# Keys and queries transposed on VectorE instead of TensorE, with values and scores set apart

## The chip, the core and the metric

The kernel runs on one core of a Trainium2 chip. The metric is the device time of one execution in microseconds (us), as the median over runs. Short names for the engines: PE is TensorE (PEld its weight loads), DVE is VectorE, ACT is ScalarE, POOL is GpSimd, SP is SyncE, whose queue issues nearly all DMAs here.

## What is computed

Batch B = 4, H = 8 heads, S = 768 tokens, D = 64 per head, all float32. First an attention in which each token sees a window of its neighbours (less than 16 away) and, for every block of 32 tokens, one summary key and one summary value; then a Fourier mixing layer with a two-layer MLP.

```python
k_sum = k.reshape(B, H, nb, 32, D).max(axis=3)
v_sum = v.reshape(B, H, nb, 32, D).mean(axis=3)
scores = concat(masked(q @ k.T / 8), q @ k_sum.T / 8 + log(32))
x = softmax(scores) @ concat(v, v_sum)            # heads side by side: (B, S, 512)
u = x + real(fft(fft(x, axis=1), axis=2))
out = u + relu(layernorm(u) @ w_ch1) @ w_ch2      # 512 -> 2048 -> 512
```

## The kernel before

**Stages.** The work goes batch by batch. For a batch b the program runs the attention (`gen_attention`, x of the batch), the Fourier mixing and normalisation (`gen_fourier`, whose result `u` holds the transposed, normalised rows) and the MLP: `gen_hidden(b, c)` (L1253) forms eight hidden layers j in two halves c, `gen_out(b, c)` (L1301) multiplies each half by the second weights. Both use a Strassen-like scheme: seven products X, Y, Z on sums and differences of quarter matrices. Matmuls named hx, hy, hz (L1268) are the hidden ones, ox, oy, oz (L1333) the output ones. Every product in float32 shows up in the trace as two passes per matmul, transposes as one.

**Overlap.** The attention of batch b+1 is spread among the MLP products of batch b. Generators do this: each `yield` ends a trip, and `drive` (main program, L1448) runs the generators by given rates: `(most, 44)` for the MLP of batch b, 74 for `gen_attention(b + 1)`. The trips give the program order; the tile framework then fixes one order per engine, in which each engine runs strictly, with semaphores for what it must wait for. The MLP of batch 0 runs beside the conversion of the weights from float64 (tiles `words`, on DVE and ACT) and beside batch 1's attention; there are four pairs of heads g per batch, and (b, g) names one.

**One pair of heads.** `load` (L574) fetches the keys and the queries of the pair, one DMA for each of the tiles kn and qn, with tokens on partitions, into a pool of four buffers (two pairs). `prepare` (L678) transposes them: for batches above 0, two groups of three PE transposes per tile (qk, L699) into PSUM, each followed by two copies on ACT (L701) into `kt` and `qt`, where partitions are the head dimension; then a block maximum of the keys on DVE (`km`, L706). `scores` (L757) makes 48 small matmuls (sc, L765), exponentials on ACT and a mask product on DVE (p); `sum_scores` (ss, L781) does the same for the block keys. `values` (L784) forms the weighted values: a small product vs (L788), which DVE spreads into the tile `vs`, 48 small matmuls (av, L798), 6 that use `vs` (L803), and on DVE a reciprocal and a scaled write into x. `load_values` fetches the values of a later pair in four DMAs (vw, 64 partitions by 12 pieces of 256 bytes); `block_sums` fetches four pieces of v (vb) into the one buffer called "room" and has POOL add them up.

In `gen_attention` (L949) a trip around the loop goes: values of the pair before, scores of this pair, both in one go; then loads; some empty trips; `prepare` of the next pair; `load` of the pair three ahead; more empty trips.

**Weights.** `get_w1` and `get_w2` fetch the seven-part weight tiles (w<-dw) two hidden layers ahead into three and four buffers. In batch 1 the first four second-weight tiles (w2 of j = 0 to 3) come with four parts only; DVE forms the other parts (four additions `w<-w`) and a DMA writes them back (dw<-w).

**PSUM.** Dense products rotate over four banks, attention over four others. An accumulating bank is read by DVE or ACT (`tt`, L566, or a copy) between two of its products, so PE waits where such a read is late: of hx, for instance, the last product of a layer needs DVE's addition `h<-hx,h` to have finished.

Of the kernel before, what the change touches and what calls it, by code (L numbers as in the profile page):

```python
# [490 lines left out]
def _main_program(ctx, tc, q, k, v, moe_w_ch1, moe_w_ch2, out):  # L491


    nc = tc.nc
    B, H, S, D = q.shape
# [5 lines left out]
    NP = H // 2  # L501
# [49 lines left out]
    def fetch(out, in_):  # L551

        ins = nc.sync.dma_start(out=out, in_=in_)
        if in_order[0]:
            tc.keep_in_program_order(ins)
# [16 lines left out]
    nat, marks = {}, {}  # L572

    def load(b, g, *which):  # L574

        for n in which or (1, 0):
            t = nat[b, g, n] = apool.tile([P, 2, NST // 2, 2 * D], FP, tag="nat", bufs=4, name=f"{'qk'[n]}n_{b}_{g}")
            fetch(out=t.rearrange("p e j n -> p (e j) n"),
                  in_=(q, k)[n][b, 2 * g:2 * g + 2].rearrange("e (j p s) d -> p (e j) (s d)", p=P, s=2))

# [60 lines left out]
    def load_values(b, g):  # L641
        if is_wide(b):
            load_wide_values(b, g)
            return
        if g % 2 and following(b, g, 1) and (b, g) != (1, 1) and not (b > 1 and g == 1):
            block_sums(*divmod((b * NP + g + 1) // 2, NP // 2))
        load_narrow_values(b, g)
# [30 lines left out]
    def prepare(b, g, *which):  # L678
        qn, kn = (nat[b, g, n] for n in range(2))
        kt, km = kt_bufs[g % 2], km_bufs[g % 2]  # L680
        qt = apool.tile([P, S], FP, tag="qt", name=f"qt_{b}_{g}") if 0 in (which or (0,)) else None
        for n in which or (1, 0):
            src, dst = (kn, kt[:, W:W + S]) if n else (qn, qt)
            if is_wide(b):
                for j0, j1 in ((0, 2), (2, 3)):
                    n = 2 * P * (j1 - j0)
                    ps = bank([P, n], f"qk_{b}_{g}_{j0}")
                    for j in range(j0, j1):
                        for s in range(2):
                            for e in range(2):  # L690
                                nc.tensor.matmul(ps[D * e:D * (e + 1), 2 * P * (j - j0) + s:2 * P * (j - j0 + 1):2],
                                                 src[:, e, j, D * s:D * (s + 1)], ident, start=True, stop=True)
                    nc.scalar.copy(out=dst[:, 2 * P * j0:2 * P * j1], in_=ps)
            else:
                for e in range(2):

                    ps = abank([P, S2], f"qk_{b}_{g}_{e}")
                    for j in range(NST // 2):
                        nc.tensor.transpose(ps[:, P * j:P * (j + 1)], src[:, e, j, :], ident)  # L699
                    for s in range(2):  # L700
                        nc.scalar.copy(out=dst[D * e:D * (e + 1), s:S:2], in_=ps[D * s:D * (s + 1)])  # L701
        if which == (0,):
            nat[b, g] = qt
            return
        with tc.issue_after(marks["fold", 0]) if (b, g) == (1, 0) else ExitStack():
            nc.vector.tensor_reduce(out=km[:, 0:nb], in_=kt[:, W:W + S].rearrange("p (n f) -> p n f", f=BLOCK),  # L706
                                    op=ALU.max, axis=AX.X)
        nat[b, g] = qt
# [48 lines left out]
    def scores(b, g):  # L757
        kt, qt = kt_bufs[g % 2], nat[b, g]
        ps = [abank([P, NB2, BLOCK], f"sc_{b}_{g}_{h}") for h in range(2)]
        for i in range(NB2):  # L760
            for h in range(2):
                o = BLOCK * (NB2 * h + i)
                for e in range(2):
                    rows, r = slice(D * e, D * (e + 1)), 64 * (e ^ h)
                    nc.tensor.matmul(ps[h][r:r + 64, i, :], kt[rows, o:o + 64], qt[rows, o:o + BLOCK],  # L765
                                     start=True, stop=True)
        p = apool.tile([P, 2, NQ, QB], FP, tag="p", name=f"p_{b}_{g}")
        pm = p[:, 1].rearrange("p n c -> p (n c)")[:, 0:S2]
        p = p[:, 0].rearrange("p (h i) (j c) -> p h (i j) c", h=2, c=BLOCK)
        for h in range(2):  # L770
            nc.scalar.activation(out=p[:, h], in_=ps[h], func=AF.Exp, scale=SC)  # L771
            tt(p[:, h], p[:, h], near[:, h], ALU.mult)
        return p, pm

    def sum_scores(b, g, p):
        km, qt = km_bufs[g % 2], nat[b, g]
        ps = abank([P, S2], f"ss_{b}_{g}")
        for h in range(2):
            for e in range(2):
                rows, r = slice(D * e, D * (e + 1)), 64 * (e ^ h) + 32 * h  # L780
                nc.tensor.matmul(ps[r:r + 32, :], km[rows, :], qt[rows, S2 * h:S2 * (h + 1)], start=True, stop=True)  # L781
        nc.scalar.activation(out=p, in_=ps, func=AF.Exp, scale=SC)
# [32 lines left out]
    def following(b, g, n):  # L815
        i = b * NP + g + n
        return divmod(i, NP) if i < B * NP else None
# [131 lines left out]
    def gen_attention(b):  # L949
        x = bpool.tile([P, NST, DM], FP, tag="x", bufs=2, name=f"x_{b}")  # L950
        x_of[b] = x
        held, pause = None, 1 if b == 1 else 5
        for g in range(NP + 1):
            if held:
                values(b, g - 1, *held, x)
            if g < NP:
                held = scores(b, g)
                sum_scores(b, g, held[1])
            if g and (n1 := following(b, g, 1)):
                load_values(*n1)  # L960
            if g == 1 and b > 1:
                block_sums(b, 1)
            if g == NP and b > 1:
                turn_tiles(b, x)
                for _ in range(12):
                    yield
                rooms[b] = room(f"fold_{b}")
                steps = fold_batch(b, split_fold(b, rooms[b]))
                while True:
                    with tc.issue_after(marks["dense"]):  # L970
                        done = next(steps, steps) is steps
                    if done:
                        break
                    yield
            if g == NP:
                return
            for _ in range(pause):
                yield
            n1, n3 = (following(b, g, n) for n in (1, 3))
            if n1 and b == 1:  # L980
                prepare(*n1)
            elif n1:
                prepare(*n1, 1)
                for _ in range(pause // 2):
                    yield
                prepare(*n1, 0)
            if n3:
                load(*n3)
            for _ in range(pause if b == 1 else pause - pause // 2):
                yield  # L990


# [396 lines left out]
    for vw in vw_bufs:  # L1389
        nc.gpsimd.tensor_copy(out=vw[:, :, D].rearrange("p (e n) -> p e n", e=2),  # L1390
                              in_=count[:, None, :].to_broadcast([P, 2, NQ]))

    def chain(*gens):
        for gen in gens:
            yield from gen
# [43 lines left out]
    for b in range(B):  # L1439


        most = chain(gen_hidden(b, 0), gen_out(b, 0), gen_hidden(b, 1))
        if b == 0:
            in_order[0] = False
            drive((most, 5, 0), (weights, 15, 0), (attn, 1, 0))
            done_weights.append(True)
        else:
            drive((most, 44, 0), (gen_attention(b + 1) if b + 1 < B else iter(()), 74, 0))  # L1448
        last = gen_out(b, 1)
        if b + 1 < B:  # L1450
            drive((gen_fourier(b + 1), 22, 600), (last, 12, 0))
        else:
            drive((last, 1, 0))
        if b == B - 2:

            ok = apool.tile([P, B * NP * 2 * NST], FP, tag="qt", name="ok")
            all_ok = spool.tile([P, 2], FP, tag="all_ok", name="all_ok")
            flag = cpool.tile([1, 1], I32, name="flag")
            rv = rec.rearrange("p n h i -> p (n h i)")
            nc.vector.tensor_scalar(out=ok, in0=rv, scalar1=1.0 / LIM, scalar2=None, op0=ALU.is_ge)  # L1460
            nc.vector.scalar_tensor_tensor(out=ok, in0=rv, scalar=LIM, in1=ok, op0=ALU.is_le, op1=ALU.mult)
            nc.vector.tensor_reduce(out=all_ok[:, 0:1], in_=ok, op=ALU.min, axis=AX.X)
            nc.vector.memset(all_ok[:, 1:2], 1.0)
            ps = bank([1, 1], "flag_ps")
            nc.tensor.matmul(ps, all_ok[:, 0:1], all_ok[:, 1:2], start=True, stop=True)
            nc.vector.tensor_scalar(out=flag, in0=ps, scalar1=P - 0.5, scalar2=None, op0=ALU.is_lt)
# [40 lines left out]
```

## Time and profile before

| | |
|---|---|
| median of 3 runs | 814.14 us (813.08 to 815.66) |
| the profiled execution | 820.64 us, of which the span in the trace is 818.8 us |
| mean granted PE clock | 0.981 of full speed |
| PE busy | 793.2 us, 97% |
| PE weight loads | 581.6 us, 71% |
| DVE busy | 492.6 us, 60% |
| ACT busy | 252.0 us, 31% |
| POOL busy | 46.2 us, 6% |
| DMA packets | 102332, 121.85 MB; 50768 under 512 bytes |
| qk transposes (L699), kn and qn | 72 each, 288 and 286 ns, 11.2 and 10.9 us busy |
| copies of them on ACT (L701) | 48 each for kt and qt, 506 and 504 ns |
| DMA issues of kn and qn | 16 each, 384 KB |

A line of the timeline reads: start in us, length of the group in us, engine, line of the program, operation, output<-inputs, shapes, and how many instructions it merges; brackets at its end hold the engine's idle time ahead of it and what released it, where "issue" means that it waited for nothing the profile shows. Matmuls are pipelined and their ends are modelled, so the spacing from start to start tells more than the length. In the DMA view, packets are single contiguous pieces; a share of 100% means that all 16 DMA engines' time is taken, and it can read above that where packets overlap.

### The profile page before, as it was taken

The page shows a single profiled execution, that of the slowest core. Times are in us where ns is not written, and L with a number is a line of the kernel's source. Part 1 is how long each engine was busy: PE and PEld are TensorE (multiplying, and loading weights), DVE is VectorE, ACT ScalarE, POOL GpSimd, SP SyncE. Part 2 cuts the span into 40 slices and gives each one's busy share as a digit, 9 for nine tenths or more (in the row PEclk, how much of TensorE's full clock was granted, in tenths as well). Part 3 has the DMA queues.
Part 4 walks back from the last instruction along what each step waited for, and adds up shares of the span by engine and source line. Part 5 has one row for each costly group of instructions (what it writes and reads, how often), then busy time and mean ns, then how long its engine had stood idle before and what let it go on. Part 6 is the DMA issues. An engine that isn't in the chain of part 4 may idle for free.

```text
span 818.8 us, 14635 instructions
## 1 busy us (share of the span) xinstructions
PE 793.2 (97%) x5998; PEld 581.6 (71%) x5998; DVE 492.6 (60%) x1121; ACT 252.0 (31%) x549; POOL 46.2 (6%) x85
## 2 busy tenths in 40 slices
PE   8969899999999999999999999999999999999997
PEld 6768665545579865688669876688659875786686
DVE  5767999887997753453577723364566723532351
ACT  3523765543635132411126114320116202001200
POOL 0010000000000310000030300000120000000000
PEclk9959999999999998999999999999999999999999
DMA  9998699788734376744614256411614044205001
GB/s 201 229 207 172 161 311 295 169 260 249 248 135 145 116 256 157 169 116 103 251 42 149 78 194 185 92 47 35 243 39 152 26 160 163 90 1 224 1 27 54
DMA packets 102332, 121.85 MB, mean 149 GB/s; under 512 B 50768, under 2 KB 83760, under 8 KB 102064
## 3 DMA queue, kind: packets, MB, share of 16 engines
q1 hardware_dynamic: 100992, 118.52, 50.2%
q0 software_dynamic: 576, 2.10, 0.8%
q8 instruction: 49, 0.80, 0.4%
q10 hardware_dynamic: 688, 0.20, 0.1%
q14 instruction: 27, 0.22, 0.1%
HBM read 97.22 MB, written 23.59 MB: 148 GB/s over the span
## 4 chain that ended last, share of the span: by engine, by line
PE 89%; DVE 4%; ACT 3%; DMA 2%; issue 1%; SPq 0%; DVEq 0%
PE hx L1268 20%; PE ox L1333 17%; PE hz L1268 10%; PE oz L1333 8%; PE o L1310 5%; PE hy L1268 5%; PE oy L1333 4%; PE y L1168 4%; PE sc L765 2%; PE mx L1127 2%; PE unt L1246 1%; PE av L798 1%; PE qk L699 1%; PE av L803 1%; PE ss L781 1%; DMA words<-in_v_dram 1%
## 5 line engine op out<-in xcount | busy, mean ns | idle before, releaser
L1268 PE MATMUL hx<-u,w 128*128 128x384 f32 x512 | 187.1, 493 | 0.3 <-ACT h L1279 0.2
L1268 PEld LDWEIGHTS hx<-u,w 128*128 128x128 f32 x512 | 95.1, 191 | 68.1 <-issue 3.6
L1268 PE MATMUL hz<-u,w 128*128 128x384 f32 x256 | 93.8, 489 | 0.0
L1333 PE MATMUL oz<-w,s 128*128 128x256 f32 x336 | 80.8, 379 | 0.0
L1333 PE MATMUL ox<-w,s 128*128 128x256 f32 x336 | 80.3, 380 | 0.0
L1333 PE MATMUL ox<-w,h 128*128 128x256 f32 x336 | 79.0, 380 | 1.0 <-DVE x L566 1.0
L566 DVE TENSOR_TENSOR x<-ox,x 128x256 f32<-128x256 f32 x84 | 35.2, 422 | 68.5 <-PE ox L1333 68.1
L1268 PEld LDWEIGHTS hz<-u,w 128*128 128x128 f32 x256 | 48.9, 192 | 34.6 <-issue 1.1
L1333 PEld LDWEIGHTS ox<-w,h 128*128 128x128 f32 x336 | 63.1, 190 | 10.5 <-DVE x L566 1.4
L1333 PEld LDWEIGHTS ox<-w,s 128*128 128x128 f32 x336 | 63.0, 190 | 9.9 <-issue 1.2
L1333 PEld LDWEIGHTS oz<-w,s 128*128 128x128 f32 x336 | 63.4, 190 | 8.7 <-DVE x L566 0.3
L1279 ACT COPY h<-hx 128x384 f32<-128x384 f32 x32 | 15.3, 479 | 143.1 <-PE hx L1268 143.0
L566 DVE TENSOR_TENSOR h<-hx,h 128x384 f32<-128x384 f32 x32 | 17.8, 555 | 55.7 <-PE hx L1268 55.7
L566 DVE TENSOR_TENSOR h<-hy,h 128x384 f32<-128x384 f32 x32 | 17.8, 555 | 50.1 <-PE hy L1268 48.1
L1268 PE MATMUL hy<-u,w 128*128 128x384 f32 x128 | 47.0, 488 | 0.6 <-issue 0.6
L1310 PE MATMUL o<-w,h 128*128 128x512 f32 x96 | 42.3, 595 | 0.0
L771 ACT ACTIVATE p<-sc 128x384 f32<-128x384 f32 x24 | 10.7, 488 | 95.1 <-PE sc L765 77.4
L1333 PE MATMUL oy<-w,h 128*128 128x256 f32 x168 | 39.9, 379 | 0.0
L1295 ACT ACTIVATE h<-hx 128x384 f32<-128x384 f32 x32 | 15.7, 491 | 70.1 <-PE hx L1268 70.0
L1268 PEld LDWEIGHTS hy<-u,w 128*128 128x128 f32 x128 | 24.0, 190 | 17.2 <-issue 1.2
L566 DVE TENSOR_TENSOR x<-oz,x 128x256 f32<-128x256 f32 x42 | 17.7, 422 | 30.1 <-PE oz L1333 29.8
L1333 PEld LDWEIGHTS oy<-w,h 128*128 128x128 f32 x168 | 31.9, 190 | 4.3
(162 smaller groups left out, 1147.1 us busy)
## 6 DMA issues: line engine op xcount, KB each, us to landing
w<-dw SPq DMA_DIRECT2D x44, 896.0 KB, 5.6
words<-in_moe_w_ch_dram SPq DMA_DIRECT2D x32, 512.0 KB, 6.1
dw<-w SPq DMA_DIRECT2D x12, 896.0 KB, 7.2
vw<-in_v_dram SPq DMA_DIRECT2D x47, 192.0 KB, 5.8
kn<-in_k_dram SPq DMA_DIRECT2D x16, 384.0 KB, 5.5
qn<-in_q_dram SPq DMA_DIRECT2D x16, 384.0 KB, 6.5
out_dram<-x SPq DMA_DIRECT2D x24, 256.0 KB, 2.5
vb<-in_v_dram SPq DMA_DIRECT2D x24, 192.0 KB, 4.2
```

Source lines behind the costliest of these rows:

```text
L566: return nc.vector.tensor_tensor(out=out, in0=in0, in1=in1, op=op).ins
L699: nc.tensor.transpose(ps[:, P * j:P * (j + 1)], src[:, e, j, :], ident)
L765: nc.tensor.matmul(ps[h][r:r + 64, i, :], kt[rows, o:o + 64], qt[rows, o:o + BLOCK], start=True, stop=True)
L771: nc.scalar.activation(out=p[:, h], in_=ps[h], func=AF.Exp, scale=SC)
L781: nc.tensor.matmul(ps[r:r + 32, :], km[rows, :], qt[rows, S2 * h:S2 * (h + 1)], start=True, stop=True)
L1127: nc.tensor.matmul(out, y[:, g], table, start=False, stop=True, skip_group_check=True)
L1168: nc.tensor.matmul(y, fgs[b][par][:, st, P * g:P * (g + 1)], fs[par][:, g % 2, st, :], start=(st == 0), stop=(st == n - 1))
L1268: ins = nc.tensor.matmul(ps, w[:, a, kk, :], u[:, r, kk, :], start=start and kk == 0, stop=stop and kk == 1, skip_group_check=True)
L1279: nc.scalar.copy(out=c11, in_=X)
L1295: nc.scalar.activation(out=c21, in_=X, func=AF.Relu)
L1310: nc.tensor.matmul(ps, h[:, n, hf, P * t:P * (t + 1)], wt[2, b, j][:, 2 * hf:2 * hf + 2, :], start=(n, hf) == (0, 0), stop=(n, hf) == (NC ...
L1333: nc.tensor.matmul(ps, left[a][:, n, :], wt[2, b, j][:, r, :], start=start and n == 0, stop=stop and n == NC - 1, skip_group_check=True)
```

## The change

From pair (2, 1) on, that is for the seven pairs (2, 1) to (3, 3):

- `load` brings each tile as four DMAs of 32 partitions, in which a partition receives 24 pieces of 32 floats (128 bytes): token 32 m + r of a head goes to partition r, block m. Each head fills two groups of 32 partitions, one for each half of its dimension.
- `prepare` turns the tile with one DVE transpose of 128 by 768 elements, which transposes each 32 by 32 block, straight into `kt` or `qt`. The PE transposes and ACT copies of these pairs go.
- Pairs (2, 1) and (2, 2) are no longer loaded during batch 1's attention but at the start of `gen_attention(2)`.
- In batches 2 and 3, values and scores of a loop turn lie three trips apart, `load_values` follows the values, and the empty trips are spread otherwise; the fold of the finished x starts after 17 trips instead of 12; the rate in `drive` is 76 instead of 74.

```diff
@@ load
+            if (b, g) > (2, 0):
+                t = nat[b, g, n] = t.rearrange("p e j n -> p (e j n)").rearrange("p (m c) -> p m c", c=32)
+                for e in range(2):
+                    for h in range(2):
+                        r, o = D * e + 32 * h, (q, k)[n][b, 2 * g + e].offset + 32 * h
+                        fetch(out=t[r:r + 32], in_=bass.AP((q, k)[n].tensor, o, [[D, 32], [32 * D, S // 32], [1, 32]]))
+                continue
@@ prepare
+            if (b, g) > (2, 0):
+                with tc.issue_after(marks["dense"]):
+                    nc.vector.transpose(out=dst, in_=src.rearrange("p m c -> p (m c)"))
+                continue
@@ gen_attention
-        held, pause = None, 1 if b == 1 else 5
+        held = None
+        if b == 2:
+            load(2, 1)
+            load(2, 2)
         for g in range(NP + 1):
+            n1, n3 = (following(b, g, n) for n in (1, 3))
             if held:
                 values(b, g - 1, *held, x)
-            if g < NP:
-                held = scores(b, g)
-                sum_scores(b, g, held[1])
-            if g and (n1 := following(b, g, 1)):
-                load_values(*n1)
-            if g == 1 and b > 1:
-                block_sums(b, 1)
+                if n1 and b > 1:
+                    load_values(*n1)
             if g == NP and b > 1:
                 turn_tiles(b, x)
-                for _ in range(12):
+                for _ in range(17):
                     yield
...
+            elif held and b > 1:
+                yield
+                yield
+                yield
+            if g < NP:
+                held = scores(b, g)
+                sum_scores(b, g, held[1])
+            if g and n1 and b == 1:
+                load_values(*n1)
+            if g == 1 and b > 1:
+                block_sums(b, 1)
+            if g == NP and b > 1:
+                return
+            yield
             if g == NP:
                 return
-            for _ in range(pause):
-                yield
-            n1, n3 = (following(b, g, n) for n in (1, 3))
-            if n1 and b == 1:
-                prepare(*n1)
-            elif n1:
-                prepare(*n1, 1)
-                for _ in range(pause // 2):
-                    yield
-                prepare(*n1, 0)
-            if n3:
+            if b > 1:
+                yield
+                yield
+            if n1:
+                prepare(*n1, *((1,) if b > 1 else ()))
+            if b > 1:
+                yield
+                yield
+                if n1:
+                    prepare(*n1, 0)
+            if n3 and not (b == 1 and n3 > (2, 0)):
                 load(*n3)
-            for _ in range(pause if b == 1 else pause - pause // 2):
+            yield
+            if b > 1:
                 yield
@@ main
-            drive((most, 44, 0), (gen_attention(b + 1) if b + 1 < B else iter(()), 74, 0))
+            drive((most, 44, 0), (gen_attention(b + 1) if b + 1 < B else iter(()), 76, 0))
```

## The prediction

> **What bounds it now.** I read the page first, engine shares and then the chain that ended last. VectorE (DVE) is busy 60%, ScalarE (ACT) 31%, so neither sets the end; TensorE (PE) does:
>
> ```profile
> PE 793.2 (97%) x5998; PEld 581.6 (71%) x5998; DVE 492.6 (60%) x1121; ACT 252.0 (31%) x549; POOL 46.2 (6%) x85
> PE 89%; DVE 4%; ACT 3%; DMA 2%; issue 1%; SPq 0%; DVEq 0%
> ```
>
> A busy share hides slow matmuls, so I took PE's timeline in the two stretches that hold the changed work, 290 to 392 us (batch 2's attention among batch 1's layers) and 481 to 579 us (batch 3's among batch 2's), and read start to start. From the first:
>
> ```profile
> 300.42 0.82 PE L699 MATMUL qk<-ident,kn 128*128 128x128 f32 x6
> 301.27 1.56 PE L1268 MATMUL hx<-u,w 128*128 128x384 f32 x4
> 302.67 0.82 PE L699 MATMUL qk<-ident,qn 128*128 128x128 f32 x6
> 303.32 1.46 PE L1268 MATMUL hx<-u,w 128*128 128x384 f32 x4
> ...
> 308.97 1.20 PE L798 MATMUL av<-vw,p 64*32 64x65 f32 x96
> 310.10 0.94 PE L803 MATMUL av<-vs,p 64*128 64x130 f32 x12
> 310.97 0.94 PE L765 MATMUL sc<-qt,kt 64*64 64x32 f32 x49
> 313.56 1.50 PE L765 MATMUL sc<-qt,kt 64*64 64x32 f32 x47 [1.65 <-issue]
> 315.00 1.50 PE L781 MATMUL ss<-qt,km 64*32 64x384 f32 x8
> 316.43 2.93 PE L1268 MATMUL hx<-u,w 128*128 128x384 f32 x4
> 319.15 2.01 PE L1268 MATMUL hz<-u,w 128*128 128x384 f32 x4
> 320.99 2.74 PE L1268 MATMUL hx<-u,w 128*128 128x384 f32 x8
> ```
>
> Two things cost PE time. Six transposes of one tile take 0.65 us (302.67 to 303.32). And at 311.9, in the middle of a score group, PE stops 1.65 us, then runs at half speed: four hidden passes take 2.72 us (316.43 to 319.15) where 1.29 is usual. It waits for no engine ("issue"). The DMA view of 312 to 316 us shows what is around it:
>
> ```profile
> DMA packets 2457, 0.63 MB, mean 158 GB/s; under 512 B 2456, under 2 KB 2456, under 8 KB 2456
> ## 3 DMA queue, kind: packets, MB, share of 16 engines
> q1 hardware_dynamic: 2456, 0.61, 127.2%
> q8 instruction: 1, 0.02, 2.2%
> ```
>
> The rings are full of 256-byte packets of values, with one fetch of instructions among them.
>
> [...] one 16 KB packet on q8; values and scores side by side are 212 passes, each with its weight load, so over 400 instructions in 4.3 us, and the stop lies inside them. [...] the array runs at half clock [...] (granted clock 0.50 from 315 to 320 us). [...]
>
> **Part 1: transposes off PE.** Seven pairs, (2,1) to (3,3), two tiles each: 14 groups of 6. At 0.65 us plus one 0.2 us bubble (300.42 to 301.27): 14 x 0.655 + 0.2 = **-9.4 us**, all on the bound engine. 56 copies of ACT go too (L701, 504 ns: 28 us), off the path; ACT has 31%.
>
> **Part 2: values and scores apart.** With four hidden products between them the burst of instructions halves. That should remove the stop: 310.97 to 323.57 is 12.60 us; the same passes at usual pace (1.53 + 0.78 + 1.29 + 1.29 + 2.58, bubble 0.1) are 7.57: **-5.0**. In the second stretch three smaller ones: 495.22 to 496.92 (1.70 for 1.29), 524.47 to 526.58 (2.11 for 1.29), 543.49 to 546.17 (2.68 for 1.53): **-2.4**. More switches between tile shapes cost 0.1 each, about six: **+0.6**.
>
> **Part 3: 14 transposes on DVE.** Nearest row: a reduction over the same 768 elements (L706, 948 ns); I take 0.95. [...] DVE has 40% idle, so 13 us of work vanish except where they stand before an eviction that PE wants. I walked the built order of DVE. In most layers PE has 1.3 us slack and a 0.95 us transpose fits. It doesn't in batch 1's layer 0. Before, that place looks so:
>
> ```profile
> 293.41 0.89 DVE L566 TENSOR_TENSOR w<-w 128x256 f32<-128x256 f32 x2 [2.61 <-DMA w<-dw]
> 297.12 0.42 DVE L566 TENSOR_TENSOR w<-w 128x256 f32<-128x256 f32 x1 [1.23 <-DMA w<-dw]
> 297.47 0.55 DVE L566 TENSOR_TENSOR h<-hy,h 128x384 f32<-128x384 f32 x1
> 298.54 2.22 DVE L566 TENSOR_TENSOR w<-w 128x256 f32<-128x256 f32 x6
> 300.67 0.55 DVE L566 TENSOR_TENSOR h<-hx,h 128x384 f32<-128x384 f32 x1
> ```
>
> DVE already waits for weights (w2) and evicts hx at 301.2; PE's next hx product, at 301.27, needs that bank and is covered only by the transposes at 300.42. In the changed order the key transpose (0.95) and its reduction (0.95) stand ahead of this eviction and three sums behind it: 301.2 + 1.9 - 1.1 = 302.0 to 302.3, while PE arrives at 300.42: 1.9 us of stop. **And the weights come later.** SP's order now has the 4th piece of vb behind an output row (280.8), so POOL's sums (5 us from its landing, 284.4) end near 289.3, and the next four vb loads wait for them in the one "room" buffer ahead of the three w2 loads, which went at 289.07 and 291.26. w2 slips by 1 to 2 us and shares the rings with 768 KB of vb: +1.4 us. Sum of the stop **+3.3**. Next, the query transpose delays the vs product that values need: DVE ends it at +3.3 after that hx, PE asks at +2.7: **+0.6**.
>
> **Part 4: w2 of j=3 later.** Its load now stands behind eight pieces and four values loads, and its four right-hand sums on DVE (4 x 0.42) behind the last values' evictions. PE runs out of products that don't need them: T1 comes 1.8 us after the values end, PE has 0.9 us of work; then the first x eviction is 0.8 us late: **+1.75**. In batch 2 there are no such sums: nothing.
>
> A stop of 3.3 us should bring the half clock as 1.65 did (that cost 3.3 beside the stop). Bounds 0 and 4; I take **+2.0**.
>
> **Part 5: the loads.** Each tile becomes four DMAs of 768 pieces of 128 bytes. Issue on SP: nearest is vw, also 768 pieces, median 645 ns, against kn's 384: 14 x (4 x 0.645 - 0.384) = 31 us more of SP, over some 350 us in which it mostly waits; bounds 16 and 60. Less than today isn't possible. Packets: vw alone (355 to 366 us, 3136 packets, 39.8% of 16 engines) costs 22 ns each, kn's 512 bytes 28. 43,008 x 22 less 10,752 x 28 ns over 16 engines is +40 us of ring time, bounds 13 and 44 ns: +16 to +99, where the share now is 0.64 and 0.43. Behind those pieces on SP stand vw and the w1, w2 loads: w1 of j=3 would go at about 310 and is wanted at 328, so cost 0, covered by the two-layer prefetch. The transposes wait for pieces issued a pair ahead. (2,1) and (2,2) move from batch 1's attention to about 215 to 268 us, where DMA share is a third: 0. Leaving batch 0's stage, which conversions on DVE feed (95 of 110 us), they free little: 0, bounds -1.5 and +1. The later fold (17 trips for 12) and the 76 for 74 shift work without adding any: 0, cover as before.
>
> **Sum.** -9.4 - 5.0 - 2.4 + 0.6 + 3.3 + 0.6 + 1.75 + 2.0 = -8.5. The profiled execution took 820.64 (span 818.8), above the median 814.14; 820.64 - 8.5 = 812.1 there, times 814.14/820.64 gives **805.7 us**.
>
> **Rivals.**
> *A, no give-back:* w2 lands in time and the key transpose hides. For it: w2 landings vary by 2 us; ACT is freer. Against: the built order. Then only Part 4 is lost: -16.2 + 1.75, 800 us.
> *B, the stop stays:* instruction fetch is hurt by four times the packets, and small pieces of keys fill the rings as vw does. For: the same view above. Against: bursts are half as long. -8.5 + 5.0, and 1 more in the second stretch: 811.5.
> *C, slower:* SP's queue. If a piece takes 1.3 us to issue or 44 ns a packet, a pair (12 DMAs) holds SP some 16 us of the 23 us between pairs, and w1 and w2 land after PE wants them. From a delay of some 10 us on (8 to use up the gain, 2 of slack) each further us is lost, in up to eight layers: 819. Against: kn lands 3.4 us after its issue when alone.
> *D, the transposes stay on PE:* excluded, the built order has 84 fewer.
>
> **Numbers.** Forecast 0.50, A 0.24, B 0.14, C 0.12. No change means within 0.3% (811.7 to 816.6), about what a measurement tells. Faster takes the forecast, A and a part of B, less their tails: 0.77; same 0.12; slower 0.11. Range 797 to 815: A with a batch-0 gain below; above, B [...].
>
> **What would show it.** L699 x60 instead of 144; a row of transposes on DVE near 950 ns; no "issue" wait in scores; a PE wait for DVE of about 3 us near the first hidden layer of batch 1, and one of 1 to 2 us near its first ox product. Wrong if PE waits for w1, if that row is above 1.7 us, or if the score stops remain.

## The result, and the profile after

The changed kernel took **810.62 us** as a median of 7 runs (809.51 to 812.00), beside 814.14 for the kernel before (813.08 to 815.66): ratio 0.9957, 95% interval 0.9943 to 0.9970, so 3.5 us faster. A second comparison gave 0.9926 (0.9895 to 0.9956), about 6 us. The forecast was 805.7, a gain of 8.4: the sign was right, the gain less than half of it in the first comparison and some 70% in the second. Rival B had named 811.5, but by another mechanism, as will be seen.

The page after: PE has 84 instructions fewer and is still the bound.

```profile
PE 781.9 (97%) x5914; PEld 571.9 (71%) x5914; DVE 500.8 (62%) x1135; ACT 224.3 (28%) x493; POOL 46.8 (6%) x85
PE 89%; DVE 5%; ACT 2%; DMA 2%; SPq 1%; issue 1%; POOL 0%; DVEq 0%; ACTq 0%; POOLq 0%
```

PE's transposes in `prepare` are down to 60 (L710 now), as forecast. The trace has 14 transposes on DVE, at the length that was estimated (0.95); the columns are duration min/median/max in ns, then first and last start:

```profile
L693 DVE STREAM_TRANSPOSE kt<-kn x7: 960/969/971, 297.1 to 520.2; 128x768 f32<-128x768 f32 x7
L693 DVE STREAM_TRANSPOSE qt<-qn x7: 958/968/971, 302.3 to 525.3; 128x768 f32<-128x768 f32 x7
```

PE's timeline after, at the place of the first timeline that the prediction shows (start, duration, engine, line, operation, count, idle time before it). L1293 is now the hidden line, L776 the scores:

```profile
294.49 1.45 PE L1293 MATMUL hx<-u,w 128*128 128x384 f32 x4
295.78 1.45 PE L1293 MATMUL hz<-u,w 128*128 128x384 f32 x4
301.00 2.93 PE L1293 MATMUL hx<-u,w 128*128 128x384 f32 x4 [3.77 <-DVE h L566]
303.72 0.53 PE L799 MATMUL vs<-vbs,sel 96*128 96x64 f32 x2
304.18 1.65 PE L809 MATMUL av<-vw,p 64*32 64x65 f32 x96
305.76 1.55 PE L814 MATMUL av<-vs,p 64*128 64x130 f32 x12
...
312.59 1.60 PE L776 MATMUL sc<-qt,kt 64*64 64x32 f32 x96
314.12 0.85 PE L792 MATMUL ss<-qt,km 64*32 64x384 f32 x8
```

Two things are to be seen. The score group of 96 runs in one piece: the stop inside it is gone. (One short stop is left in the last score group of batch 3, 0.36 us at 532.45; in the four profiles of the kernel before that group has one of 0.39 to 0.94.) And PE now waits 3.77 us for DVE's `h` in batch 1's first hidden layer, and runs at half pace until 307 (granted clock 0.50 from 300.2 to 307.0; the hidden group spans 2.93 for 1.45, av 1.65 for 1.20). The forecast had 3.3 us and 2.0 us there. DVE's timeline at the same place, against that of before:

```profile
292.00 1.95 DVE L566 TENSOR_TENSOR w<-w 128x256 f32<-128x256 f32 x2 [4.55 <-DMA w<-dw]
293.87 1.81 DVE L566 TENSOR_TENSOR p<-p,near 128x384 f32<-128x384 f32 x2
295.60 1.08 DVE L566 TENSOR_TENSOR w<-w 128x256 f32<-128x256 f32 x3
296.61 0.54 DVE L566 TENSOR_TENSOR h<-hy,h 128x384 f32<-128x384 f32 x1
297.07 0.96 DVE L693 STREAM_TRANSPOSE kt<-kn 128x768 f32<-128x768 f32 x1
...
298.20 0.93 DVE L717 TENSOR_REDUCE km<-kt 128x24 f32<-128x768 f32 x1
299.06 1.41 DVE L566 TENSOR_TENSOR w<-w 128x256 f32<-128x256 f32 x4
300.40 0.54 DVE L566 TENSOR_TENSOR h<-hx,h 128x384 f32<-128x384 f32 x1
```

DVE idles 4.55 us for w2, then has not a moment free until the eviction (the read that empties the bank) at 300.40. The first pair of sums takes 1.95 us where it took 0.89 before.

The DMA view of 312 to 316 us after shows what the scores now run beside:

```profile
DMA packets 231, 1.11 MB, mean 279 GB/s; under 512 B 71, under 2 KB 71, under 8 KB 231
```

71 small packets instead of 2456: the values' pieces are already through.

**Where the time lies.** Cut at the first scores of batch 2, the first hidden product of batch 1's second half, the first scores of batch 3 and the first hidden product of batch 2's second half, all as starts on PE, the traces of the kernels below give (us; from the last cut to PE's last matmul it is 233.9 to 234.0 in each):

| kernel, profiled execution | up to first scores | stretch 1 | between | stretch 2 |
|---|---|---|---|---|
| before (the prediction's) | 290.26 | 102.01 | 88.90 | 97.65 |
| before, 2nd | 287.91 | 98.54 | 89.83 | 97.94 |
| before, 3rd | 285.99 | 98.51 | 88.77 | 97.55 |
| before, 4th | 287.63 | 100.20 | 88.76 | 98.02 |
| changed | 286.91 | 100.91 | 89.84 | 92.45 |
| changed, 2nd | 286.62 | 101.01 | 89.83 | 92.52 |
| order_only | 289.45 | 97.63 | 88.76 | 96.11 |
| turns_only | 311.08 | 103.01 | 89.83 | 93.99 |
| turns_moved | 284.85 | 105.82 | 89.83 | 93.99 |
| vb_late | 286.59 | 95.75 | 89.83 | 92.46 |
| big_in_four | 286.48 | 93.72 | 89.86 | 91.81 |
| sums_later, 2nd | 285.87 | 91.79 | 89.84 | 92.20 |

Against the mean of the four of before, the change is +1.1 in stretch 1, +0.8 between and -5.3 in stretch 2: **-3.4**. To that come -0.8 behind PE's last matmul, which have nothing to do with PE: the program's end, with its row of waits on SP, takes 6.0 us in the kernel before, order_only and big_pieces and 5.3 in the kernels that load these tiles by four DMAs. That makes -4.2, between the two timed gains. The part ahead of the first scores varies by 4 us among executions of one kernel, and the one from which the prediction was made is the longest of the four there and in stretch 1.

### The profile page after: what moved, and what is told of

Its sections match the earlier page's. It is cut to its first block, busy times and chain, and to the rows that moved or that the text cites. A ratio compares the mean times of both kernels' runs of the same rounds, so it can differ in the third digit from the quotient of the medians.

```text
span 809.3 us, 14447 instructions
## 1 busy us (share of the span) xinstructions
PE 781.9 (97%) x5914; PEld 571.9 (71%) x5914; DVE 500.8 (62%) x1135; ACT 224.3 (28%) x493; POOL 46.8 (6%) x85
## 4 chain that ended last, share of the span: by engine, by line
PE 89%; DVE 5%; ACT 2%; DMA 2%; SPq 1%; issue 1%; POOL 0%; DVEq 0%; ACTq 0%; POOLq 0%
PE hx L1293 20%; PE ox L1358 17%; PE hz L1293 10%; PE oz L1358 9%; PE o L1335 5%; PE hy L1293 5%; PE oy L1358 4%; PE y L1193 3%; PE sc L776 2%; PE mx L1152 2%; PE av L814 1%; PE av L809 1%; PE unt L1271 1%; DVE w L566 1%; SPq L553 1%; PE qk L702 1%
## 5 line engine op out<-in xcount | busy, mean ns | idle before, releaser
L1293 PE MATMUL hx<-u,w 128*128 128x384 f32 x512 | 187.2, 493 | 3.8 <-DVE h L566 3.8
L1293 PEld LDWEIGHTS hx<-u,w 128*128 128x128 f32 x512 | 95.7, 191 | 72.3 <-DVE h L566 5.7
L1293 PE MATMUL hz<-u,w 128*128 128x384 f32 x256 | 93.2, 487 | 0.0
L1293 PEld LDWEIGHTS hz<-u,w 128*128 128x128 f32 x256 | 48.5, 190 | 34.0 <-ACT h L1311 0.5
L1293 PE MATMUL hy<-u,w 128*128 128x384 f32 x128 | 46.7, 488 | 0.0
L1293 PEld LDWEIGHTS hy<-u,w 128*128 128x128 f32 x128 | 24.1, 190 | 16.3
L1335 PEld LDWEIGHTS o<-w,h 128*128 128x128 f32 x96 | 18.1, 190 | 21.9 <-issue 20.6
```

The costliest lines, as they stand in the source:

```text
L1293: ins = nc.tensor.matmul(ps, w[:, a, kk, :], u[:, r, kk, :], start=start and kk == 0, stop=stop and kk == 1, skip_group_check=True)
L1335: nc.tensor.matmul(ps, h[:, n, hf, P * t:P * (t + 1)], wt[2, b, j][:, 2 * hf:2 * hf + 2, :], start=(n, hf) == (0, 0), stop=(n, hf) == (NC ...
```

## The experiments

### Is the stop in the scores the program's? Three more profiles of the kernel before

> The kernel before, unchanged, profiled a second time. Theory 'part 2' (the prediction's): the stop inside the scores of batch 1's MLP and the half clock after it belong to the program, so PE again waits over 1 us for no engine between 305 and 325 us, then runs hidden passes at half pace, and the span is near 818. Rival 'accident': they belong to that one profiled execution, whose 820.64 us lay 6.5 above the median; now no such wait over 0.5 us there, no half clock near 315, and also less than the 17 us of half clock that stood at 44 to 61 us; span near 812.

> The kernel before, profiled a third time. Theory 'not every execution' (the stop of 1.5 to 1.9 us inside the scores of batch 1's MLP is the program's, the half clock behind it is not): the stop is there again, the half clock behind it may be or not, and with half clock there the span is some 3 us longer. Rival 'program': half clock follows the stop here and in the next run, and before_again was the exception.

> The kernel before, profiled a fourth time, with the same two expectations: a stop of 1.5 to 2 us near 310 us; 'program' says half clock for 6.8 us behind it, 'not every execution' says not always.

They took 815.99, 812.58 and 816.47 us. PE's timelines of the second and of the fourth at the scores:

```profile
308.61 0.94 PE L765 MATMUL sc<-qt,kt 64*64 64x32 f32 x49
310.88 0.90 PE L765 MATMUL sc<-qt,kt 64*64 64x32 f32 x47 [1.33 <-issue]
311.71 0.85 PE L781 MATMUL ss<-qt,km 64*32 64x384 f32 x8
312.49 1.56 PE L1268 MATMUL hx<-u,w 128*128 128x384 f32 x4
```

```profile
310.72 1.36 PE L765 MATMUL sc<-qt,kt 64*64 64x32 f32 x47 [1.43 <-issue]
312.01 1.50 PE L781 MATMUL ss<-qt,km 64*32 64x384 f32 x8
313.44 1.99 PE L1268 MATMUL hx<-u,w 128*128 128x384 f32 x4
```

The stop is in every execution, at the same instruction (49 of 96), and costs 1.5 to 1.9 us start to start. The half clock behind it is not: none in the second and third, 3.4 us in the fourth, 6.8 us in the first (granted clock 0.50 from 313.42 to 320.25). Stretch 1 without stop or half clock is 98.54 - 1.54 = 97.0. The mean of four exceeds that by 2.8, not by 5.0. So "not every execution" stands, and the stop itself is no accident.

The same traces show where the stops lie. I numbered PE's instructions (matmuls, weight loads and its queue's own) in order of start. The stop above ends at instruction 5313; those of stretch 2 in the kernel before end at 9154 and 9666; those of turns_moved (below) at 5313, 5826, 6338, 8386 and 8897; the short one left in the changed kernel at 9409. All are multiples of 256 apart, to within one instruction. The profiles of the kernels in this document have 30 waits of PE for "issue" of over 0.3 us after their first 100 us, and all 30 are at such places; ahead of each, a 16 KB packet of q8, as the prediction's DMA view shows one, had ended 1.24 to 1.75 us before PE went on. The view lists q8's packets as "instruction"; the kernel before has 49 of them for 12145 instructions of PE, numbered as above, and the changed one 48 for 11962, so one for 248 and 249. From these places and counts I take the stop to be a fetch of PE's next instructions that comes too late.

### Order alone

The changed order, loads of (2,1) and (2,2) moved as in the change, but these blocks left out:

```diff
-            if (b, g) > (2, 0):       # load: four DMAs of 128-byte pieces
-                ...
-            if (b, g) > (2, 0):       # prepare: nc.vector.transpose
-                ...
```

> The changed kernel with its order (values and scores as trips apart, loads of (2,1) and (2,2) from batch 1's first layer on), but transposes and loads of keys and queries as before: on PE, from 512-byte pieces. Theory 'part 2': the removed stops are worth 5.0 + 2.4, more switches cost 0.6, so 807 to 808 us. Rival 'accident': no stop was there to remove in a usual execution, so 813 to 816: the switches' +0.6 and up to 1 for the reduction of keys that now stands ahead of the first hidden eviction of batch 1.

812.54 us beside 814.64, ratio 0.9975 (0.9950 to 1.0000). No stop is left in the scores of either stretch: 97.63 and 96.11, which is 2.2 and 1.7 less than the mean of before. So the order is worth 3.9 us by the traces (the loads that move with it are ahead of these stretches), and the timed interval, 0 to 4.1 us, holds that but by itself hardly tells it from nothing. It lies between the two expectations, because the stop is real and its half clock is not regular.

### VectorE transposes in the old order

turns_only is before with the change's `load` and `prepare` blocks and nothing else; turns_moved takes the loads of (2,1) and (2,2) to batch 1's first layer as well:

```diff
+        if b == 2:
+            load(2, 1)
+            load(2, 2)
...
-            if n3:
+            if n3 and not (b == 1 and n3 > (2, 0)):
                 load(*n3)
```

> The kernel before with its order, but keys and queries from (2,1) on loaded in 128-byte pieces and transposed by VectorE. The key transpose of (2,1) stands behind the first hidden evictions of batch 1 here. Theory 'place' (the give-back is where the transpose stands among VectorE's work, not the transpose itself): 14 groups of 0.655 go, and PE waits about 0.8 us near the first hidden layer since the old transposes no longer cover the sums of w2: 814.1 - 9.2 + 0.8 = 805.7. Rival 'any VectorE transpose costs' (loads or VectorE's time give back wherever it is put): 810 to 812, as in the changed kernel.

838.91 us, ratio 1.0277 (1.0242 to 1.0311): 24 us slower, where 805.7 was expected. The table puts it ahead of the first scores, in batch 0's MLP. DVE's conversions there starve. The views by windows, with columns PE, PEld, DVE, ACT and POOL busy, clock, DMA share and GB/s, of the second profile of before and then of turns_only:

```profile
160.00:180.00 20.00, 20.00 (x124) 9.92 (x123) 16.58 (x35) 10.23 (x18) 0.00 (x0) 1.00 0.89 275
200.00:220.00 20.00, 20.00 (x62) 11.37 (x61) 19.40 (x43) 12.78 (x25) 0.00 (x0) 1.00 0.70 236
```

```profile
160.00:180.00 20.00, 20.00 (x57) 9.63 (x56) 8.55 (x16) 7.87 (x14) 0.00 (x0) 1.00 0.45 92
200.00:220.00 20.00, 20.00 (x63) 11.71 (x62) 9.26 (x21) 10.15 (x21) 0.00 (x0) 1.00 0.55 144
```

In these two stretches DVE has 8.55 and 9.26 us of work where it had 16.58 and 19.40 (not in each: between them, from 180 to 200 us, it has 17.78 for 14.93; from 100 to 260 us it is 126 for 140), while the DMA share falls. Its input, the weight words, is issued on the queue that now holds the pieces:

```profile
184.65 5.00 SPq L553 DMA_DIRECT2D kn<-in_k_dram  x4
189.75 2.18 SPq L553 DMA_DIRECT2D qn<-in_q_dram  x4
...
204.06 17.13 SPq L553 DMA_DIRECT2D words<-in_moe_w_ch_dram  x2
```

Later PE waits for `w`, which these words feed (3.87 us at 227, 3.48 at 255, 1.93 at 258). This is the kind of loss that rival C of the prediction describes, from the queue, but at a place that the change does not use.

> Before's order with VectorE transposes from 128-byte pieces, as in turns_only, but the pieces of (2,1) and (2,2) loaded from batch 1's first layer on, as the changed kernel does it. Theory 'queue' (what cost turns_only its 24 us was the pieces standing among the loads of batch 0's weights): the 24 us go and the 14 groups' 9.2 show: 814.1 - 9.2 + 0.8 = 805 to 806; the stops inside the scores stay (1.5, 1.0, 1.1 us). Rival 'VectorE': the transposes among the evictions cost it, so it stays above 812.

819.27 us beside 816.86, ratio 1.0022 (1.0003 to 1.0042). That loss is gone, so moving the loads is what makes the small pieces possible. But the 9.2 us do not show, and "place" fails as I had put it: the key transpose stands behind the hidden eviction here, and the stop is there all the same. As in the changed kernel, DVE's w2 sums start late there, 5.71 us behind the first scores, and the first pair takes 1.83 us.

```profile
298.85 4.54 PE L1282 MATMUL hx<-u,w 128*128 128x384 f32 x8 [3.69 <-DVE h L566]
...
309.36 1.13 PE L776 MATMUL sc<-qt,kt 64*64 64x32 f32 x62
312.57 0.71 PE L776 MATMUL sc<-qt,kt 64*64 64x32 f32 x34 [2.08 <-issue]
```

Stops inside the scores of stretch 1 are three now, 2.30, 1.24 and 0.78 us start to start, where before had one of 1.5 to 1.9. The second and third stand at blocks of 256 instructions (5826 and 6338) that the kernel before passes without such a stop. With small pieces beside them the undivided values and scores are hurt more. That speaks for rival B's late fetches, and the changed order keeps all but the short one at 532 us out of the changed kernel.

### The sums of w2

sums_later leaves the changed kernel's loads as they are and issues the right-hand sums of w2, j = 0 to 3 in batch 1, at the end of each hidden layer; before_sums_later does the same to the kernel before:

```diff
         if b == 1 and j < NC:
             fetch(out=w[:, 0:4], in_=dw2[j][:, 0:4])
-            _right_sums(tt, lambda i: w[:, i])
-            fetch(out=dw2[j][:, 1:7], in_=w[:, 1:7])
...
+            if b == 1 and j < NC:          # gen_hidden, after the last eviction of layer j
+                with tc.issue_after(marks["dense"]):
+                    sum_w2(j)              # the two lines taken out above
```

> The changed kernel, but the right-hand sums of w2 in batch 1's first half are issued at the end of each hidden layer, behind its evictions, not at its start. Theory 'place': the wait of PE for the hx eviction in batch 1's layer 0 (3.8 us) and the half clock behind it (2.7) go, and so does the wait at the first ox product of batch 1 (about 1.3): 810.6 - 7.7 = 803 us. Rival 'queue': the key transpose and the reduction alone still delay that eviction or the loads delay something else: 807 to 810.

> The changed kernel with the right-hand sums of w2 at each layer's end, once more, beside the others: ratio 0.978 to 0.984 if the first measurement stands; 0.986 or more would say that it caught a favourable set of runs.

> The kernel before, with the right-hand sums of w2 in batch 1's first half moved to the end of each hidden layer. Theory 'place': in the kernel before PE never waited for that eviction, so nothing is gained, 813 to 815. Rival 'sums cost anywhere': the gain of sums_later is not the change's give-back taken away but a gain of its own: 806 to 810 here too.

sums_later, in two comparisons: 801.43 and 802.65 us, ratios 0.9811 (0.9780 to 0.9842) and 0.9847 (0.9813 to 0.9881); the second lies between its two expectations. Stretch 1 is 91.79, with no PE wait over 0.4 us in it: the stop, the half clock and the wait at the first ox product are gone, 100.96 - 91.79 = 9.2 us in all. In the kernel before the same edit gains nothing, 1.0025 (1.0003 to 1.0047). So what it gains is the change's give-back, that is, what the change loses again in stretch 1. These sums are the common load on DVE; they don't say yet what pushed them against the eviction.

### Loads or transpose?

after_again is the changed kernel again. big_pieces and big_in_four load 512-byte pieces, in one and in four DMAs per tile (the latter by the lines with c):

```diff
-            if (b, g) > (2, 0):                 # load: the four DMAs of 128-byte pieces
-                ...
+            for r in range(0, P, 32 if (b, g) > (2, 0) else P):
+                c = slice(r, r + (32 if (b, g) > (2, 0) else P))
+                fetch(out=t.rearrange("p e j n -> p (e j) n")[c],
+                      in_=(q, k)[n][b, 2 * g:2 * g + 2].rearrange("e (j p s) d -> p (e j) (s d)", p=P, s=2)[c])
```

vb_late keeps everything but four loads. They are the second group of vb in front of w2; the prediction counted them without asking whose they are. They are batch 3's block sums, issued that early because their buffer was free:

```diff
-        ... and (b, g) != (1, 1) and not (b > 1 and g == 1):
+        ... and (b, g) not in ((1, 1), (2, 3)) and not (b > 1 and g == 1):
             block_sums(*divmod((b * NP + g + 1) // 2, NP // 2))
...
+        if b == 3:                          # gen_attention
+            block_sums(3, 0)
```

> The changed kernel, unchanged, beside the other three and profiled again. If its first trace is typical, the ratio to before is again near 0.9957 (810 to 811 where before is 814) and PE again waits over 3 us for the hx eviction of batch 1's layer 0, with half clock after it. If that stop was an accident of the first profile, the wait is under 2 us and the ratio below 0.990.

> The changed kernel, but keys and queries loaded in the old 512-byte pieces, so that VectorE transposes tiles that are laid out differently: scores from (2,1) on are of other data, the amount of work is the same. It prices the 128-byte pieces. Prediction's Part 5 (cost 0): as the changed kernel, ratio 0.994 to 0.998. Rival 'packets': the 32,000 packets more and 21 more issues delay w2 or values somewhere on the path: 3 us or more below the changed kernel, ratio 0.992 or less.

> As big_pieces (512-byte pieces, so scores from (2,1) on are of other data), but each tile loaded by four DMAs of 32 partitions, as many as in the changed kernel. It parts the number of DMAs from the size of the pieces. Theory 'number': SP's queue with four DMAs per tile puts the block sums' loads behind output rows, so the stop of about 4 us at batch 1's layer 0 returns: ratio 0.991 to 0.996. Rival 'size': the small packets fill the rings; with large ones the stop stays near 1.1 us: ratio 0.984 to 0.988.

> The changed kernel, but the four loads of batch 3's first block sums (they are not wanted before batch 3's attention, yet stand ahead of w2 on SP) go to the start of batch 3's attention; VectorE's order in batch 1's layer 0 stays as it is. Theory 'loads' (about 3 us of the 4.1 us stop are w2 landing late and GpSimd's sums of those blocks slowing VectorE's): w2 lands about 3 us after the first scores instead of 5.3, the stop shrinks to some 1.1 us, the half clock of 2.7 goes: 810.4 - 3 - 2.7 = 804 to 805, ratio 0.985 to 0.988. Rival 'transpose' (the key transpose and its reduction ahead of the eviction make the stop): it stays above 3 us, ratio 0.992 to 0.996.

| kernel | us | ratio (95%) | w2 sums start, from first scores | stop, start to start |
|---|---|---|---|---|
| after_again | 810.39 | 0.9926 (0.9895 to 0.9956) | +5.36 | 4.12 |
| big_pieces | 804.50 | 0.9854 (0.9814 to 0.9895) | +3.02 | 1.08 |
| big_in_four | 803.36 | 0.9856 (0.9825 to 0.9886) | +3.14 | 1.64 |
| vb_late | 805.79 | 0.9882 (0.9851 to 0.9913) | +3.28 | 1.36 |

(The second profile of before has +2.98 and no stop.) The changed kernel's stop is in each of its profiles. With nothing but those four loads moved, it falls from 4.12 to 1.36 and the half clock goes. DVE's timeline of vb_late, in the same order of instructions:

```profile
289.87 0.88 DVE L566 TENSOR_TENSOR w<-w 128x256 f32<-128x256 f32 x2 [2.75 <-DMA w<-dw]
290.67 1.02 DVE L566 TENSOR_TENSOR p<-p,near 128x384 f32<-128x384 f32 x2
```

The two rows that took 1.95 and 1.81 take 0.88 and 1.02. POOL's timelines show what stood beside them: in the changed kernel it adds up batch 3's blocks at that very time (first fence); in vb_late its sums had ended at 283.8 (second).

```profile
287.42 1.27 POOL L569 TENSOR_TENSOR vb<-vb 96x512 f32<-96x512 f32 x1 [3.44 <-DMA vb<-in_v_dram]
290.99 4.27 POOL L569 TENSOR_TENSOR vb<-vb 96x512 f32<-96x512 f32 x4 [2.31 <-DMA vb<-in_v_dram]
```

```profile
283.52 0.32 POOL L569 TENSOR_TENSOR vbs<-vb 96x64 f32<-96x64 f32 x1
```

So 1.1 us are lost on the first pair of sums (1.95 for 0.88) and 0.8 on the pair after it (1.81 for 1.02), both of SBUF tiles alone, against POOL additions of 1.07 us each (four in 4.27). In the second profile of sums_later a key transpose and an addition `h<-hy,h`, which reads PSUM, run beside the same GpSimd sums at 0.97 and 0.56 us, as elsewhere. The runs show the lost time and its company; what the two engines contend for they don't show.

"Loads" therefore holds: about 2.8 us of the 4.1 us stop and the half clock, and 1.1 to 1.6 is left. That this rest is the transpose and the reduction is by subtraction (order_only, which has the reduction there and PE's transposes to cover it, stops 0.46 us). Timed, 0.9882 lies at the edge of what "loads" expected, and its interval overlaps that of 0.9926; by the traces stretch 1 is 5.2 us shorter. "Number" fails: four DMAs of large pieces leave a stop of 1.64. It is the size of the pieces, but not because small packets fill the rings at that place: vb_late keeps them, and its stop is short. It is what the size does to the order of SP's queue. In the profile of big_in_four SP issues vb in one go at 267.23, with all pieces of (2,2) out by 241.5; in the second profile of the changed kernel pieces of (2,2) stand at 247 to 266, and vb behind output rows:

```profile
267.23 1.76 SPq L553 DMA_DIRECT2D vb<-in_v_dram  x4
```

```profile
264.44 1.67 SPq L553 DMA_DIRECT2D qn<-in_q_dram  x3
268.43 0.32 SPq L553 DMA_DIRECT2D vb<-in_v_dram  x1
273.78 0.36 SPq L553 DMA_DIRECT2D out_dram<-x  x1
274.18 0.90 SPq L553 DMA_DIRECT2D vb<-in_v_dram  x2
275.96 0.36 SPq L553 DMA_DIRECT2D out_dram<-x  x1
276.36 9.26 SPq L553 DMA_DIRECT2D vb<-in_v_dram  x5
```

That order is fixed when the program is built; both profiles of the changed kernel have it. Of those five, four wait in SP until POOL has done with the buffer (276.36 to 285.6), and w2 comes next. But w2 is hardly issued later for that, as its first loads in the changed kernel (second profile) and in vb_late show:

```profile
285.67 0.43 SPq L553 DMA_DIRECT2D w<-dw  x1
```

```profile
285.39 0.34 SPq L553 DMA_DIRECT2D w<-dw  x1
```

It lands later. From 286 to 288 us the DMA engines are 99% taken in the changed kernel, where the four vb loads have just been issued, and 60% in vb_late. In the first profile of the changed kernel it is 105%, and w2's 4 KB packets, from 287.40 on, come behind the 2 KB ones of vb, from 284.94 on.

### Both mends

> sums_later and the later block sums together. Either alone takes the stop of batch 1's layer 0, so little is left for both: 'place' and 'loads' expect the ratio of sums_later, 0.981, less 0 to 1 us: 0.979 to 0.982. Rival: loads that move to batch 2's end cost there what they give here: 0.984 or more.

801.96 us, ratio 0.9818 (0.9781 to 0.9854). Once the edit of sums_later has taken the stop, that of vb_late adds nothing that can be measured. Both beat the kernel before and the changed one; sums_later alone is the smaller edit.

## Why the prediction was right and wrong

**Part 1, -9.4: right.** From order_only to sums_later the stretches lose 5.84 and 3.91, so -9.75 for the 14 groups, with a stop of 0.46 us in order_only that goes with them. By stretch it fits too: 8 groups of 0.655 and that stop are 5.7, 6 groups are 3.9.

**Part 2, -6.8 net: the step that failed.** The traces of order_only show -3.9. The first term, -5.0, was start to start of one execution; the stop in it, 1.5 to 1.9, is regular, the rest was half clock that two of four executions don't have. The mean of the four is 2.8 above a stretch without either. In the second stretch the order was worth 1.7, where -2.4 and a part of the +0.6 was put. The 0.1 for a switch of tile shapes can be read in the changed kernel: behind the block scores or the values a hidden group takes 1.40 us start to start for 1.29 (314.90 to 316.30, 326.30 to 327.70), ahead of the scores 1.38 (311.21 to 312.59). I had noted that the profiled execution was 6.5 us above the median, and scaled the sum by 0.8% for that. What was needed was the question which of the terms makes it so long. That 812.1 was forecast for a profiled execution and 811.17 was measured is luck: the typical execution of before had less to lose. Of the 5.1 us between the -8.5 of the sum and the -3.4 of the stretches, Part 2 is 2.9, the next paragraph 1.5 and the stretch between 0.8.

**Part 3, half clock and Part 4: 7.65 forecast, 9.2 measured.** The stop for `h` stood where it was expected, 3.93 and 4.12 start to start for 3.3. The wait for vs, put at 0.6, did not come: vs follows at 303.72 without one. Half clock cost 2.7 (from 301.00 to the next layer's hx at 307.24 it is 6.24 us; the same products take 3.55 in sums_later) for 2.0. The waits at the first output products were 1.28 for 1.75. About 1.2 is left; in this stretch PE changes from one product to another 74 times, in sums_later 66 times, which was not measured apart. But the composition of the stop was wrong: 1.9 was put down to transpose and reduction, 1.4 to w2. The runs show 2.8 for w2 and the block sums, and leave 1.1 to 1.6 for the rest. Of w2's two reasons, the later issue by 1 to 2 us did not come (its first load goes 1.1 us ahead of the first scores, 1.2 before), the shared rings did. GpSimd's sums beside VectorE's were not in the working at all.

**Part 5, cost 0: wrong for the small pieces.** By themselves the pieces are cheap: in 299.0 to 303.2 us of the changed kernel's trace 3161 packets take 62.3% of 16 engines, 13 ns each, and four issues take 2.15 us, 0.54 each. Their real price is that they move other loads: big pieces make the changed kernel 0.7% faster (0.9854 against 0.9926). The 0 for taking the loads out of batch 0's stage is not refuted: the part ahead of the first scores is 289.45 in order_only, inside the 285.99 to 290.26 of the kernel before. What I had not asked is what the small pieces would do if they stayed there: 2.5% (1.0277 against 1.0022), some 21 us.

**What I had not seen**, +0.8 between the stretches: DVE's sums of u (three, 2.69 us in the first profile of before) take 3.76 where POOL's block sums run beside them, and PE then stands still 0.93 us for `x`. One of four profiles of before shows it, and all of the kernels with VectorE transposes. What shifts the two against each other stays open.

**Rivals.** A needed w2 in time, which it was not. With w2 out of the way (sums_later) the kernel takes 801 to 803, and A had said 800. B gave the nearest number for the wrong reason: the stop did not stay. A loss from SP's queue, as in C, happened in turns_only, not in the changed kernel.

That the stop in the scores is a late fetch of instructions was argued in the prediction from the one packet of q8 beside it; the places of the stops, 256 instructions or a multiple apart and 1.24 to 1.75 us behind such a packet, now support it. Dividing values from scores takes the large stops away (one of 0.36 us is left in the changed kernel's scores), and with smaller pieces beside them the undivided ones have more (three in turns_moved's stretch 1, where the kernel before has one). Why a fetch comes late at one block and in time at another stays open.

## What to carry to other kernels

A loss that is read from one profiled execution is worth its mean over executions: profile twice before you count a stop's aftermath as gain, above all when that execution is longer than the median. When transfers are cut smaller, look through the built order of their queue for what they push back, and price that, not the packets. An eviction on an engine's in-order queue is best kept clear of sums that nobody wants yet.

## What the runs showed of the hardware

- A float32 transpose of 128 x 768 on VectorE takes 0.96 to 0.97 us, from SBUF to SBUF.
- In the four profiles of the kernel before, PE fell to half clock (granted 0.50) behind stops of 1.65 and 1.43 us, for 6.83 and 3.4 us, and not behind stops of 1.33 and 1.27; in the changed kernel's first profile it did so behind one of 3.77, for 6.83. What decides between them was not shown.
- PE's waits for "issue" of over 0.3 us, after the first 100 us, stand 256 instructions, or a multiple, apart: 30 of 30, each 1.24 to 1.75 us behind the end of a 16 KB packet on q8.
- VectorE additions of two SBUF tiles took longer beside GpSimd additions: two of 128 x 256 1.95 us (2.39 in the second profile) for 0.88, three of 128 x 768 3.76 for 2.69.
